# A planner of an attention block's engine order gets a new cost for changes of tiling, and its constants are refitted

## The chip, the cores and the metric

The kernel runs on one core of one Trainium2 chip. The metric is device time in microseconds (us); before the change it is 821.35, the median of three runs from 821.32 to 821.77. Profile times are those of one profiled execution, whose span is 820.3 us.

## The reference

One transformer block with adaptive layer norm. S = 2048 tokens, D = 640, 32 heads of 20 columns, an inner width F = 1536. The conditioning vector c gives six vectors of 640 (shift, scale and gate for each half of the block).

```python
mod = (silu(c) @ w_mod).reshape(1, 6, 1, -1)
sa, ca, ga, sb, cb, gb = (mod[:, i] for i in range(6))
h = layernorm(x) * (1 + ca) + sa
q, k, v = heads(h @ wqkv)                      # 32 heads of 20
p = softmax(einsum('bhqd,bhkd->bhqk', q, k) * 20 ** -0.5)
x = x + ga * (merge(p @ v) @ wo)
h = layernorm(x) * (1 + cb) + sb
x = x + gb * (((h @ w_gate) * (h @ w_up)) @ w_down)
```

The large part is the attention: 32 heads x 2048 x 2048 exponentials.

## The kernel before

**A planner in the kernel file.** Nothing of the order of instructions is written out by hand. `build_kernel` makes some thousands of `Task` objects (engine, assumed duration, dependencies, priority, gate, buffers to acquire), and `Sched.run` plays them forward in an assumed time: whenever an engine is free it takes the ready task of lowest priority number. `pick_pe` decides for TensorE (PE). The order that results is emitted as five fixed instruction streams with semaphore waits (`emit_program`). So a constant of the planner does no work on the chip; it moves instructions.

**Units of attention.** The queries are cut into `CHUNKS` of 512, 512, 512, 256 and 256; a chunk and a set of four heads are an item (8 items a chunk, 40 in all). A unit is one head, 128 keys and 512 queries (256 keys and 256 queries in the last two chunks). PE computes its scores into one PSUM bank (`unit_score_emits`, L1306): the head dimension lies on 32 rows of the array (row tile `32*s` for head s of the set), so units of different heads can share a pass and units of the same head can't. Then come the exponentials, in one of two ways:

- A units go to ScalarE (ACT), L1342: two units to an instruction, from group `HEADG` = 600 on alternately two and three. Two PSUM sets (banks 0 to 2, and 3 and 4) are used in turn, so the scores of a group wait until the exponential two groups back is done. The results go to the buffers PP, `NPS` = 4 of each of two kinds.
- D units go to VectorE (DVE) in quads of four: one L1366 each (scores to int16 in DB0), then three instructions for the quad (L1398, L1403, L1406) that make two terms in DSS, each of which goes through the PV product. `QUADS` says how many quads each item has. Their scores are attached to an A group (`d_attach`), up to `EAGER` units ahead of being due.

**PV products.** `pv_issue` (L1832) multiplies PP or DSS with the values, four heads side by side in column tiles, into one bank (`BPV`). An item's bank is read by DVE (the stream transpose L1486) before the next item may begin, and ends in the columns `OcT` and `Ocp` for the output projection.

**The rest of PE's work** is cut into rounds (`Round`): transposes of the normalised input (`hT_rounds`, L948), projections of K and Q (`kq_round`, L981, and `packed_round`, L1033), of V (`v_round`), and for each finished chunk the suffix: output projection (`op`), second layer norm on DVE and GpSimd, transposes (L1604), gate and up products (`g`, `u`), down projection (`dn`). Most of them record their matmuls in L827 (four column tiles) or L823 (the whole array, in the last chunk's suffix). They are slipped in between the scores by priority and gate (`need`, `K_LEAD`, `KD_LEAD`, `LATE_A`, `LATE_L`, `GATE_F`). Where the planner sees PE idle too long, it puts in a filler pass (L2101, L2103), an idle product[...].

**Changes of tiling.** Scores use row tiles (mode S), PV and most projections column tiles (mode P), transposes the whole array (mode X). `mode_start` adds the cost of a change of mode:

```python
def mode_start(mode, t):
    if sc.pe_mode is not None and sc.pe_mode != mode:
        return max(t, sc.pe_end + PE_SWITCH)
    return max(t, sc.pe_end)
```

**Stealing.** `Sched.steal` lets ScalarE take an evacuation from DVE's list when it sees no exponential due within `STEAL_GAP`, up to `STEAL_END`.

Of the kernel before, what the change touches and what calls it, by code (L numbers as in the profile page):

```python
# [14 lines left out]
PE_SWITCH = 100.0  # L15
# [10 lines left out]
STEAL_GAP = 188.158  # L26
# [402 lines left out]
QUADS = [(0, 4, 3, 3, 4, 3, 4, 3), (3, 4, 3, 4, 3, 4, 3, 4), (3, 4, 3, 4, 3, 4, 3, 4), (1, 2, 1, 2, 1, 2, 1, 2), 1]  # L429
# [3 lines left out]
EAGER = 4  # L433
# [5 lines left out]
PVTOL = 400  # L439
# [13 lines left out]
K_LEAD = 0.642  # L453
K_ALL = (0,)
KD_LEAD = 0.704
DMA_WINDOW = 900000
D_LATE = 12
D_RES = 84
# [4 lines left out]
TAILX = 1  # L463
PV0N = 1
# [13 lines left out]
HT_L = 0.046  # L478
V_L = 0.251
LATE_A = 1.114  # L480
LATE_L = 2.959
LATEQ = (3,)
LATEQ_A = 0
# [13 lines left out]
def build_kernel(nc, A_x, A_wqkv, A_wo, B_x, B_w_gate, B_w_up, B_w_down, c, w_mod, out):  # L497
# [265 lines left out]
    def load_rest():  # L763
        chain(load_w, d_wk, 0, 1, wk_sb, 0, "sp", 0.5)
        chained.append(d_wk[0])
        for q, f in enumerate((lambda: chain(load_x, 1, 0, "sp", 0.6), lambda: chain(load_w, d_wq, 0, 0, wq_sb, 0, "sp", 0.7),
                               lambda: chain(load_x, 1, 1, "sp", 0.8), lambda: chain(load_w, d_wv, 0, 2, wV, 0, "sp", 0.9),
                               lambda: chain(load_x, 2, 0, "sp", 4), lambda: chain(load_x, 2, 1, "sp", 4.1),
                               lambda: chain(load_x, 3, 0, "sp", 5), lambda: chain(load_x, 3, 1, "sp", 5.1),
                               lambda: chain(load_w, d_wk, 1, 1, wk_sb, 0, "sp", 8),  # L770
                               lambda: chain(load_w, d_wq, 1, 0, wq_sb, 0, "sp", 8.1),
                               lambda: chain(load_w, d_wv, 1, 2, wV, 0, "sp", 8.2))):
            n = len(sc.every)
            f()
            chained.append(sc.every[n])
# [17 lines left out]
    class Round:  # L793
        def __init__(self, mms, deps, after, prio, gate=0, name="", banks=None, pdeps={}):
# [11 lines left out]
            for i, (dur, f) in enumerate(mms):  # L806
                t = Task("pe", dur, wrap(f), deps if i == 0 else pdeps.get(i, ()), ctr="pex", prio=prio, gate=gate, name=name,
                         mode="P" if isinstance(f, list) else "X")
                if i > 0:
                    follower[id(self.tasks[-1])] = t  # L810
                self.tasks.append(t)
# [8 lines left out]
            self.evac[-1].on_start = lambda task: banks.done(b["b"], task)  # L820
# [120 lines left out]
    def hT_rounds(tc, prio):  # L941
        s2 = tc % 2
        t_hT[tc] = []
        tr_last[tc] = []
        for k in range(KD):
# [18 lines left out]
    kt_ready = {}  # L964
    qt_ready = {}
# [9 lines left out]

    def kq_round(kind, j, tc, prio, gate=0):
# [8 lines left out]
        pieces = [(ci, q0 % 512, n) for ci, (q0, n) in enumerate(CHUNKS) if q0 // 512 == tc]  # L985

        def after(r):
            if kind == "K":
                dps = [r_sb.last, r_cb.last] if j >= 4 else []
                f = lambda e: e.tensor_copy(KT[:, j, tc * 512:(tc + 1) * 512], bank(r.b["b"]))  # L990
                fa = lambda e: e.copy(KT[:, j, tc * 512:(tc + 1) * 512], bank(r.b["b"]))
                return [evac(512, ps_cost(512), f, fa, [r.last] + dps)]
            ts = []
            for ci, so, n in pieces:
                f = lambda e, ci=ci, so=so, n=n: e.tensor_scalar(QT[ci][:, j, :], ps[:, r.b["b"], so:so + n], qcol[:, 0:1],
                                                                 None, op0=ALU.mult)
                fa = lambda e, ci=ci, so=so, n=n: e.activation(QT[ci][:, j, :], ps[:, r.b["b"], so:so + n], AFT.Copy,
                                                               scale=qcol[:, 0:1])
                ts.append(evac(n, ps_cost(n), f, fa, [r.last] + d_q + (x0_done if ci > 0 else [])))
            return ts  # L1000
# [5 lines left out]
        r = Round(mms, list(t_hT[tc]) + w_deps(kind, j) + xd, after, prio, gate=gate, name=f"{kind}{j}.{tc}")  # L1006
        if kind == "K":
            kt_ready[(j, tc)] = [r.evac[0]]
        else:
            for (ci, so, n), t in zip(pieces, r.evac):  # L1010
                qt_ready[(j, ci)] = [t]
# [15 lines left out]
    def packed_round(kind, b, tc, prio, gate=0, late_q=False):  # L1027
# [24 lines left out]
        r = Round(mms, list(t_hT[tc]) + dw, after, prio, gate=gate, name=f"{kind}p{b}.{tc}")  # L1052
# [54 lines left out]
    def v_round(t, pt, prio, gate=0):  # L1107
# [14 lines left out]
        r = Round(mms, list(t_hT[t // 4]) + [d_wv[a // 4]], after, prio, gate=gate, name=f"V{t}.{pt}")  # L1122
# [174 lines left out]
    def unit_score_deps(u):  # L1297
        d = list(qt_ready[(u.j, u.ci)])
        for tc in sorted(set(kt // 4 for kt in u.kts)):
            d += kt_ready[(u.j, tc)]  # L1300
        return d
# [452 lines left out]
    def mode_start(mode, t):  # L1754
        if sc.pe_mode is not None and sc.pe_mode != mode:
            return max(t, sc.pe_end + PE_SWITCH)
# [82 lines left out]
    def pv_issue(cands, t):  # L1839
# [4 lines left out]
        w = 216.0 * clk()  # L1844
# [60 lines left out]
    def pick_x(t, warm=False):  # L1905
# [3 lines left out]
        if xcur[0] is not None:  # L1909
            cand = xcur[0]  # L1910
            if any(d.done is None or d.done + SEM > t for d in cand.deps):
                return False
# [12 lines left out]
        if cand is not None:  # L1925
# [8 lines left out]
            xcur[0] = follower.get(id(cand))  # L1934
            return True
# [46 lines left out]
    def pick_pe(t):  # L1982
# [67 lines left out]
        if cands:  # L2050
# [4 lines left out]
            if PVTOL and sr is not None and not force:  # L2055
                k = int((sr + PVTOL - mode_start("P", t)) // 216.0)
# [62 lines left out]
    def fill_ok(t, fdeps):  # L2119
        if any(d.done is None or d.done + SEM > t for d in fdeps):  # L2120
            return False
        if xcur[0] is not None:
            return False
# [3 lines left out]
    xcur = [None]  # L2127
    sc.pick_pe = pick_pe
# [47 lines left out]
```

## Time and profile before

| | before |
|---|---|
| time | 821.35 us (821.32 to 821.77) |
| span of the profiled run | 820.3 us, granted TensorE clock 1.00 |
| exponentials on ScalarE (L1342) | 779 instructions, the first at 15.9 us, the last ends at 785.5 us |
| scores (L1306) | 2560 matmuls |
| DVE's share of the exponentials | 400 units: 265.5 us in L1366, 121.9 in L1403, 69.7 in L1398, 68.0 in L1406 |
| filler passes in column tiles (L2103) | 244 matmuls, 21.6 us |

Busy times are of one execution. Matmuls overlap, so PE's busy time says that something was under way and not that the array was full; a matmul that is recorded with 0.39 us can follow the one before it by 0.22. An idle time in square brackets stands before the instruction and names who ended it. The exponentials of 1024 elements are recorded with 1124 ns on average, but overlap each other: their distance from start to start is what counts.

### The profile page before, as it was taken

The numbers are of one execution on the slowest core, as the hardware profiler recorded it, in microseconds if no ns is written. First come the engines' busy times: TensorE is split into PE (matmuls) and PEld (weight loads), VectorE is DVE, ScalarE is ACT, GpSimd is POOL, SyncE is SP. The second block draws the span as 40 slices with busy tenths as digits, with TensorE's granted clock in tenths as the row PEclk, the third lists the DMA queues.
The fourth block names the chain that finished last, engine by engine and source line by source line (L and its number), as shares of the span: only waits on it lengthen the run. The fifth ranks groups of instructions, "written<-read, shape, count | busy, mean of one in ns | idle before, by whom it ended". The sixth has DMA issues, their size and how long they took to land.

```text
span 820.3 us, 27666 instructions
## 1 busy us (share of the span) xinstructions
PE 796.5 (97%) x11894; PEld 297.1 (36%) x11894; DVE 727.9 (89%) x1276; ACT 775.6 (95%) x822; POOL 71.7 (9%) x104
## 2 busy tenths in 40 slices
PE   9999999999999999999999999999999999999998
PEld 4433233322232222223333222223344443454567
DVE  7889899999899999999999999999789898758663
ACT  6889999999999999999999999999999999999931
POOL 2300000000001000000002000000011000001000
PEclk9999999999999999999999999999999999999999
DMA  9452311124400125100310121100401226106420
GB/s 294 128 169 71 95 50 41 33 66 131 111 15 26 44 64 155 41 5 15 70 42 6 37 46 46 37 5 19 102 5 30 62 66 136 31 30 141 104 59 17
DMA packets 115895, 54.23 MB, mean 66 GB/s; under 512 B 83771, under 2 KB 115775, under 8 KB 115775
## 3 DMA queue, kind: packets, MB, share of 16 engines
q1 hardware_dynamic: 114847, 51.33, 24.4%
q8 instruction: 94, 1.54, 0.8%
q10 hardware_dynamic: 928, 1.15, 0.4%
q14 instruction: 26, 0.21, 0.1%
HBM read 41.75 MB, written 8.41 MB: 61 GB/s over the span
## 4 chain that ended last, share of the span: by engine, by line
PE 42%; ACT 35%; DVE 14%; issue 7%; DMA 1%; SPq 0%; POOL 0%; ACTq 0%; DVEq 0%; POOLq 0%
ACT PP L1342 35%; PE ps_all L1306 13%; PE ps_all L827 13%; PE ps_all L1832 9%; DVE DB L1366 5%; PE ps_all L823 3%; PE ps_all L1033 2%; DVE DSS L1403 1%; DVE DSS L1398 1%; DVE DSS L1406 1%; PE ps_all L2101 1%; DVE st L921 1%; PE ps_all L981 1%; DVE wd L1294 1%; DVE hprod L1690 0%
## 5 line engine op out<-in xcount | busy, mean ns | idle before, releaser
L1342 ACT ACTIVATE PP<-ps_all 128x1024 bf16<-128x1024 f32 (+1 forms) x779 | 756.5, 1166 | 7.8 <-PE ps_all L1306 4.9
L1306 PE MATMUL ps_all<-QT,KT 32*128 32x512 bf16 (+1 forms) x2560 | 320.6, 339 | 12.8 <-ACT PP L1342 7.9
L1366 DVE TENSOR_SCALAR DB<-ps_all 128x512 int16<-128x512 f32 x400 | 265.5, 684 | 32.1 <-PE ps_all L1306 30.3
L1306 PEld LDWEIGHTS ps_all<-QT,KT 32*128 32x128 bf16 x2560 | 85.3, 91 | 277.2 <-ACT PP L1342 239.3
L1832 PE MATMUL ps_all<-PP,Vf 128*32 128x512 bf16 (+2 forms) x2080 | 163.4, 343 | 0.1
L1403 DVE TENSOR_TENSOR DSS<-DB,DSS 128x2048 bf16<-128x2048 bf16 x100 | 121.9, 1219 | 0.0
L827 PE MATMUL ps_all<-h2T,stg 128*32 128x512 bf16 x1440 | 116.0, 382 | 1.1 <-DVE DB L1366 0.4
L1491 POOL TENSOR_TENSOR OTn<-OT,invT 128x512 bf16<-128x512 f32 (+1 forms) x39 | 39.7, 1017 | 617.6 <-DVE invT L1489 617.6
L1832 PE MATMUL ps_all<-DSS,Vf 128*32 128x512 bf16 (+1 forms) x960 | 78.7, 347 | 0.1
L1832 PEld LDWEIGHTS ps_all<-PP,Vf 128*32 128x32 bf16 (+1 forms) x2080 | 46.5, 94 | 87.2 <-issue 80.6
L1398 DVE TENSOR_SCALAR DSS<-DB 128x2048 int16<-128x2048 int16 x100 | 69.7, 697 | 0.7
L1406 DVE TENSOR_SCALAR DSS<-DB 128x2048 int16<-128x2048 int16 x100 | 68.0, 680 | 0.8 <-PE ps_all L1832 0.7
L827 PE MATMUL ps_all<-wd,hprod 128*32 128x320 bf16 x1152 | 58.4, 301 | 0.2 <-DVE DB L1366 0.2
L827 PEld LDWEIGHTS ps_all<-h2T,stg 128*32 128x32 bf16 x1440 | 31.1, 95 | 34.6 <-issue 23.2
L1679 DVE CAST gsb<-ps_all 128x512 bf16<-128x512 f32 (+1 forms) x48 | 29.7, 619 | 5.8 <-PE ps_all L827 5.4
L827 PEld LDWEIGHTS ps_all<-wd,hprod 128*32 128x32 bf16 x1152 | 27.2, 96 | 18.4 <-issue 8.8
L1832 PEld LDWEIGHTS ps_all<-DSS,Vf 128*32 128x32 bf16 x960 | 25.1, 95 | 20.6 <-issue 8.8
L827 PE MATMUL ps_all<-wV,hT 128*32 128x320 bf16 x640 | 31.4, 301 | 0.1
L1033 PE MATMUL ps_all<-hT,wq 128*32 128x512 bf16 x375 | 31.1, 382 | 0.0
L1486 DVE STREAM_TRANSPOSE OT<-ps_all 128x512 f32<-128x512 f32 (+1 forms) x40 | 24.3, 606 | 7.7 <-PE ps_all L1832 7.4
L827 PE MATMUL ps_all<-wo,Ocp 128*32 128x320 bf16 x560 | 30.6, 301 | 0.4 <-DVE DB L1366 0.4
L1498 DVE STREAM_TRANSPOSE OcT<-OTn 128x512 bf16<-128x512 bf16 (+1 forms) x40 | 23.8, 596 | 2.2 <-POOL OTn L1491 2.2
(123 smaller groups left out, 519.5 us busy)
## 6 DMA issues: line engine op xcount, KB each, us to landing
stg<-in_B_w_gate_dram SPq DMA_DIRECT2D x50, 160.0 KB, 2.8
stg<-in_B_w_up_dram SPq DMA_DIRECT2D x50, 160.0 KB, 3.0
QT<-q_rows SPq DMA_DIRECT2D x22, 128.0 KB, 2.9
KT<-k_rows SPq DMA_DIRECT2D x84, 32.0 KB, 1.7
wm<-in_w_mod_dram SPq DMA_DIRECT2D x3, 800.0 KB
x<-in_A_x_dram SPq DMA_DIRECT2D x7, 320.0 KB
xck<-in_A_x_dram SPq DMA_DIRECT2D x3, 640.0 KB
wd<-in_B_w_down_dram SPq DMA_DIRECT2D x1, 1920.0 KB
```

The source lines that it names most:

```text
L823: return lambda e, b: e.matmul(ps[:, b, c0:c0 + n], lhs(), rhs(), start=st, stop=sp)
L827: return lambda e, b: e.matmul(ps[32 * x:32 * x + 32, b, c0:c0 + n], lhs()[:, 32 * x:32 * x + 32], rhs(), tile_position=(0, 32 * x), start ...
L1033: f = [lambda e, b_, k=k, x=x: e.matmul(ps[x:x + min(32, w - x), b_, :], wx[:, k, r0 + x:r0 + min(x + 32, w)], hT[tc][:, k, :], tile_posit ...
L1306: ems.append(lambda e, i=i, kt=kt: e.matmul(dstf()[:, i * u.n:(i + 1) * u.n], KT[32 * u.s:32 * u.s + 32, u.j, kt * 128:(kt + 1) * 128], QT ...
L1342: return e.activation(PPs[g % 2][:, cellp["p"], 0:nu * 512], ps[:, b0:b0 + nu, :].rearrange("p b c -> p (b c)"), AFT.Exp, scale=ESCALE)
L1366: return e.tensor_scalar(DB0[:, st_["slot"], x * 512:(x + 1) * 512], bank(cell["b"]), EBIAS, 0.0, op0=ALU.add, op1=ALU.max)
L1398: return e.tensor_scalar(DSS[:, st_["ss"][0], :], DB0[:, st_["slot"], :], 0x7F, 0x3F00, op0=ALU.bitwise_and, op1=ALU.bitwise_or)
L1403: return e.tensor_tensor(d, DB0[:, st_["slot"], :].bitcast(BF16), d, ALU.mult)
L1406: return e.tensor_scalar(DSS[:, st_["ss"][1], :], DB0[:, st_["slot"], :], 0x7F80, 2, op0=ALU.bitwise_and, op1=ALU.bitwise_or)
L1491: f3 = lambda e: e.tensor_tensor(OTn[:, 0:n].rearrange("p (b c) -> p b c", c=32), OT[:, 0:n].rearrange("p (b c) -> p b c", c=32), invT[:, ...
L1679: f = lambda e: e.tensor_copy(gsb[:, gs, 0:n], ps[:, r.b["b"], 0:n])
L1832: ems.append(lambda e, i=i, kt=kt, stt=stt, stp=stp: e.matmul(ps[32 * s:32 * s + mc, BPV, 0:u.n], Vf[:, (kt * H + 4 * u.j + s) * VW:(kt * ...
```

## The change

The planner's cost of a change of tiling is split in two: leaving the scores' row tiles costs `PE_BACK` = 112 ns, any other change `PE_SWITCH` = 102 ns (both were 100). The duration of a pass of PV products becomes a constant (`PV_W`, still 216 ns), and an extra for the first pass of a round is prepared (`X_FIRST`, 0). Several new ways of ordering are built in and left off (`PASSDEP`, `WQ_FIRST`, `EV_SPLIT`, `HT0_SPLIT`, `PREEMPT`). One new path is live: when the next pass of a round that has begun is blocked, small `col` matmuls may go ahead of it. The other constants are fitted again to the planner so changed. Among them are two that change the work itself: the item pattern `QUADS` has two quads fewer in the fourth chunk (12 become 10), and in the second chunk the sixth item has one quad less and the seventh one more.

```diff
-PE_SWITCH = 100.0
+PE_SWITCH = 102.0
+PE_BACK = 112.0
+PV_W = 216.0
+X_FIRST = 0.0
...
-STEAL_GAP = 188.158
+STEAL_GAP = 138.041
...
-QUADS = [(0, 4, 3, 3, 4, 3, 4, 3), (3, 4, 3, 4, 3, 4, 3, 4), (3, 4, 3, 4, 3, 4, 3, 4), (1, 2, 1, 2, 1, 2, 1, 2), 1]
+QUADS = [(0, 4, 3, 3, 4, 3, 4, 3), (3, 4, 3, 4, 3, 3, 4, 4), (3, 4, 3, 4, 3, 4, 3, 4), (1, 2, 1, 2, 1, 1, 1, 1), 1]
...
-EAGER = 4
+EAGER = 7
...
-PVTOL = 400
+PVTOL = 300
...
-K_LEAD = 0.642
+K_LEAD = 0.686
 K_ALL = (0,)
-KD_LEAD = 0.704
+KD_LEAD = 0.64
 DMA_WINDOW = 900000
 D_LATE = 12
-D_RES = 84
+D_RES = 79
...
+PASSDEP = 0
+WQ_FIRST = 0
+EV_SPLIT = 0
+PASS_TC = (0, 1, 2, 3)
+HT0_SPLIT = 0
+PREEMPT = 0.0
+PRE_M = 0.3
...
-HT_L = 0.046
+HT_L = 0.11
 V_L = 0.251
-LATE_A = 1.114
-LATE_L = 2.959
+LATE_A = 2.37
+LATE_L = 2.957
 LATEQ = (3,)
-LATEQ_A = 0
+LATEQ_A = 4
...
-            return max(t, sc.pe_end + PE_SWITCH)
+            return max(t, sc.pe_end + (PE_BACK if sc.pe_mode == 'S' else PE_SWITCH))
...
-                k = int((sr + PVTOL - mode_start("P", t)) // 216.0)
+                k = int((sr + PVTOL - mode_start("P", t)) // PV_W)
```

## The prediction

> **What bounds the kernel now.** I read the page first, then the busy time of each engine by stretch, then the exponentials alone, then the waits and the timeline where the exponentials thin out. The page:
>
> ```profile
> PE 796.5 (97%) x11894; PEld 297.1 (36%) x11894; DVE 727.9 (89%) x1276; ACT 775.6 (95%) x822; POOL 71.7 (9%) x104
> ...
> PE 42%; ACT 35%; DVE 14%; issue 7%; DMA 1%; SPq 0%; POOL 0%; ACTq 0%; DVEq 0%; POOLq 0%
> ```
>
> PE looks like the bound, in busy time and in the chain that ended last. The waits say otherwise:
>
> ```profile
> PEld ps_all L1306 <- ACT PP L1342: 239.3, 639, 1.1
> ```
>
> 639 weight loads of score groups (0.37 us each on average) wait for ScalarE to let go of a PSUM pair. So over most of the span PE follows ScalarE. The exponentials by stretch (stretch, length, ACT busy, count):
>
> ```profile
> 16.00:72.00 56.00, 46.64 (x51) 1.00 0.49 143
> 72.00:119.00 47.00, 46.44 (x52) 1.00 0.31 79
> 119.00:166.00 47.00, 46.02 (x51) 1.00 0.14 40
> 166.00:560.00 394.00, 393.91 (x431) 1.00 0.19 50
> ...
> 680.00:780.00 100.00, 99.95 (x89) 1.00 0.41 90
> ```
>
> A stretch counts an exponential that straddles its edge, so I take one off. Undisturbed, one of two units starts every 0.904 us (the chain has six in 5.41 us at 220). From 16 to 72 some 50 start: 56 - 50 x 0.904 = 10.8 us lost. From 72 to 166 about 3 us are lost, from 166 to 560 394 - 430 x 0.904 = 5.3 us, or 1.4%. From 680 to 780, where groups of two and three units alternate, 88 start in 100 us, 0.45 us a unit. So ScalarE is the bound from about 70 to 785 us; before that it starves, and the timeline shows what it starves for, and one more hole later on:
>
> ```profile
> 37.17 7.44 ACT L1342 ACTIVATE PP<-ps_all 128x1024 bf16<-128x1024 f32 x8 [1.45 <-PE ps_all L1306]
> 45.47 3.77 ACT L1342 ACTIVATE PP<-ps_all 128x1024 bf16<-128x1024 f32 x4 [0.86 <-PE ps_all L1306]
> ...
> 621.30 79.82 ACT L1342 ACTIVATE PP<-ps_all 128x1024 bf16<-128x1024 f32 x70 [1.83 <-PE ps_all L1832]
> ```
>
> The first two are scores that PE brings late, behind projections. The third waits for PV products to free PP buffers, and PV waits for DVE to read the finished item out of its bank:
>
> ```profile
> 601.06 0.45 DVE L1486 STREAM_TRANSPOSE OT<-ps_all 128x256 f32<-128x256 f32 x1
> ...
> 620.34 0.45 DVE L1486 STREAM_TRANSPOSE OT<-ps_all 128x256 f32<-128x256 f32 x1
> ```
>
> Between these two item ends lie 19.3 us in which DVE hardly pauses. After the last exponential (785.5) PE works without a break to the end, but for one hole:
>
> ```profile
> 792.59 3.44 PE L827 MATMUL ps_all<-wd,hprodt 128*32 128x320 bf16 x96
> ...
> 795.96 0.73 PE L1604 MATMUL ps_all<-ident,xn2c 128*128 128x128 bf16 x10
> ```
>
> The gate product behind it waits 1.12 us for h2Tc and starts at 797.82.
>
> **What the Trainium skill says.** "ScalarE: Activation LUTs" (What ACT_TABLE_LOAD costs) gives 0.833 ns an element plus 186 ns, with 93 ns of overlap back to back: 946 ns for 1024 elements. The trace has 0.904 us, and I use the trace. "TensorE: Matmul & The Clock Gate" (The mechanism, in Part 3) lets matmuls at different row positions overlap in the array. The trace agrees: the scores of different row tiles cost one pass, while two units on one row tile cost a second one:
>
> ```profile
> 45.03 0.61 PE L1306 MATMUL ps_all<-QT,KT 32*128 32x512 bf16 x5
> 45.57 0.40 PE L1832 MATMUL ps_all<-PP,Vf 128*32 128x512 bf16 x4
> ...
> 46.77 0.39 PE L1306 MATMUL ps_all<-QT,KT 32*128 32x512 bf16 x3
> 47.09 0.73 PE L827 MATMUL ps_all<-wV,hT 128*32 128x320 bf16 x16
> ```
>
> From score start to next start: 0.54 us with five units, 0.32 with three, so 0.22 us a repeated pass. "TensorEngine Tiling (Array Packing)" (Key Properties) says that a change of tiling mode drains the array. 0.32 less a 0.216 us pass leaves about 0.1 us a change, as both planners assume.
>
> **The change part by part**, from the order of instructions in the two built programs and the durations above.
>
> *Constants of the switch, and switches left off.* The planner's costs set no instruction. The new paths (split evacuation, dependencies by pass, split transposes) are off, and changes of tiling number 1567 before and 1568 after. By themselves they cost 0: what counts is the order that comes out.
>
> *Two quads fewer in the fourth chunk.* Eight units move from DVE to ScalarE, 1648 + 400 becoming 1656 + 392: 691 exponentials of two units (689 before), 91 of three (90), one of one. 8 x 0.45 = **+3.6 us** on ScalarE, in a stretch in which it has no gap. DVE loses 2 x (4 x 0.684 + 1.219 + 0.697 + 0.680) = 10.7 us, off the path: ScalarE's exponentials hide it. PE loses two passes of PV, 0.4 us, hidden likewise.
>
> *Fewer repeated score passes.* 834 passes become 798: 36 x 0.216 = 7.8 us of PE. Most lie where ScalarE sets the pace (units 600 to 1400), and ten more filler passes there (71 against 61, 2.2 us) show that PE merely has more room. Groups with a repeated pass start their exponential only some 10 to 20 ns later than others do. Together with the quad moved from the sixth to the seventh item of the second chunk, where DVE is busy 39.89 of the 40 us from 320, I give the saturated stretch **-1.0 us** of its 5.3 (bounds 0 and 2.5).
>
> *Order of the head.* Up to the first PV the orders are the same. From there transposes, V and K projections are dealt differently. Adding pass times and 0.107 us a change of tiling ahead of each exponential, PE brings the 100th ScalarE unit 0.5 us earlier, the 160th to 270th 1.7 to 2.5 us, the 280th to 300th 1.0 to 1.3 us. PE sets the pace there, so ScalarE gains what PE does: **-2.0 us** (bounds 0.5 and 3).
>
> *The hole at 621.* Between the same two item ends DVE now has one DB evacuation less (0.68), one sum (0.48), one normalisation (0.44), one aggregation (0.2) and two h2T evacuations (1.0), which come after: 2.8 us less than 19.3. The PV products come that much earlier, and the hole of 1.83 closes: **-1.8 us** (bounds 0 and 1.8, as the same 28 PV products are still piled up behind it).
>
> *Tail.* 12 passes of down projection move from ahead of the output projection to between the transposes and the first gate product: 12 x 0.14 = 1.7 us that cover the 1.12 us hole and a little more. Queued behind them on PE are the gate products alone, which could not start anyway. From the last PV product to the first gate product there were 22 down passes (3.1), the output projection (3.4), 24 down passes (3.4), the transposes (0.6) and 1.2 of hole, 11.7 in all; now 2 up passes (0.2), 12 down, the output projection, 24 down, the transposes, 12 down, 11.0: **-0.7 us** (bounds -1.1 and 0).
>
> *Waits and releases.* ScalarE steals the same evacuations as before; two V evacuations now stand together (0.42 us each), while PE is the bound: 0.
>
> Sum: 3.6 - 1.0 - 2.0 - 1.8 - 0.7 = -1.9 us, so 821.35 - 1.9 = **819.4 us**.
>
> **The rivals.**
> (a) *Nearly no change*: the head gains only the 1.3 us of its latest late unit (280 to 300), the hole closes by half, the saturated stretch yields nothing: 3.6 - 1.3 - 0.9 - 0.7 = +0.7, 822.0. For it speaks that a wait which is removed early is paid again if a later unit is late.
> (b) *Slower*: exponentials are added for certain, and the stalls stay, since the same item end piles up the same 28 PV products and a second pile of 24 follows 26 units later where there was none: 3.6 - 0.7 - 0.5 = +2.4, 823.8. For it speaks that ScalarE is the bound by every stretch; against it, that DVE's work ahead of the pile is less.
> (c) *Larger gain*: PE is the bound after all, as the 97% suggest. Its counted work falls 7.8 + 0.4 - 2.2 = 6.0 us: 815.4. Against it speak the 639 waits for ScalarE.
>
> **How the numbers follow.** Forecast 0.40, (a) 0.23, (b) 0.24, (c) 0.13. Faster by over 0.2% (below 819.7) are the forecast and (c): 0.53. Slower (above 823.0) is (b): 0.24. The range runs from (c) to (b), 815.4 to 823.8; beyond it lie half of (c) on one side and less than half of (b) on the other. All single terms at their best or worst would give 816.5 and 824.5, and they will hardly all fall together.
>
> **What would show it.** Right: the last exponential ends about 784.3 (785.5 - 1.2), the count from 16 to 72 rises by one or two, no ScalarE gap over 1 us near 620, no PE hole ahead of the first gate product. Wrong: the same 10.8 us lost before 72, a gap near 620 as long as before or a new one some 12 us later, or exponentials in the saturated stretch further apart than 0.914 us, which would be ScalarE waiting on a PE that holds fewer, larger bundles.

## The result, and the profile after

The changed kernel takes **824.63 us** (median of six runs, 824.28 to 826.0) beside 821.66 (821.32 to 821.93) for the kernel before on the same chip: a ratio of 1.0038, 95% interval 1.0026 to 1.0051. It is slower by 0.26% to 0.51%, above the range of 815.4 to 823.8, where 819.4 had been forecast. The span of the profiled execution is 822.5 us, 2.2 more than before (the profiled execution of before was a run of 822.43 us, 0.8 above its median; that of after one of 824.28).

The page of the changed kernel, busy times and the chain that ended last:

```profile
PE 791.9 (96%) x11918; PEld 292.7 (36%) x11918; DVE 719.2 (87%) x1262; ACT 778.2 (95%) x826; POOL 77.7 (9%) x104
...
PE 41%; ACT 40%; DVE 11%; issue 7%; DMA 1%; ACTq 0%; DVEq 0%
```

and from its waits (us in total, times, longest) the largest of the score groups:

```profile
PEld ps_all L1373 <- ACT PP L1409: 259.4, 678, 0.9
```

PE is 4.6 us less busy, DVE 8.7 less, ACT 2.6 more, and 678 score loads instead of 639 wait for ScalarE. By these numbers PE has more room, and the kernel is slower. The exponentials by stretch (stretch, length, ACT busy, count):

```profile
16.00:72.00 56.00, 46.15 (x50) 1.00 0.49 144
72.00:119.00 47.00, 46.83 (x52) 1.00 0.28 74
119.00:166.00 47.00, 44.78 (x49) 1.00 0.15 43
...
560.00:621.00 61.00, 61.00 (x59) 1.00 0.15 37
621.00:680.00 59.00, 59.00 (x53) 1.00 0.25 56
```

Up to 166 us 151 exponentials against 154 before. Forecast was one or two more up to 72; there is one fewer. From 560 to 680 ScalarE is busy all 120 us: the hole is gone. ScalarE's timeline shows both, here the starved parts of the head and the last stretch:

```profile
58.12 1.94 ACT L1409 ACTIVATE PP<-ps_all 128x1024 bf16<-128x1024 f32 x2 [0.20 <-PE ps_all L1899]
60.55 1.94 ACT L1409 ACTIVATE PP<-ps_all 128x1024 bf16<-128x1024 f32 x2 [0.50 <-PE ps_all L1899]
...
151.32 1.94 ACT L1409 ACTIVATE PP<-ps_all 128x1024 bf16<-128x1024 f32 x2 [0.39 <-PE ps_all L1899]
154.28 1.02 ACT L1409 ACTIVATE PP<-ps_all 128x1024 bf16<-128x1024 f32 x1 [1.03 <-PE ps_all L1899]
...
482.58 305.16 ACT L1409 ACTIVATE PP<-ps_all 128x1024 bf16<-128x1024 f32 x290 [0.38 <-PE ps_all L1373]
```

In the last line 290 exponentials run on to 787.7 with no gap worth a line of its own. The waits of the head shown here have another releaser than the two shown of before: L1899 is the PV product, not the score product (L1373). ScalarE has its scores and waits for a PP buffer. Its waits over the first 166.5 us (us in total, times, longest), two lines of before and then two of after, say the same for the whole head:

```profile
ACT PP L1342 <- PE ps_all L1306: 4.9, 7, 1.4
ACT PP L1342 <- PE ps_all L1832: 0.5, 2, 0.3
...
ACT PP L1409 <- PE ps_all L1899: 4.1, 9, 1.0
ACT PP L1409 <- PE ps_all L1373: 3.2, 6, 1.4
```

The waits for scores fell by 1.7 us, about what was forecast for the head, and the waits for PV products rose by 3.6.

**The ledger.** I laid the start of every exponential of both traces side by side, by the ScalarE unit it begins with. The column "trace" is how much (after - before) grows over each part:

| part | forecast, us | trace, us |
|---|---|---|
| head, to unit 300 | -2.0 | +1.1 |
| units 300 to 1200, saturated | -1.0 | -0.1 |
| units 1200 to 1300, the hole | -1.8 | -1.9 |
| units 1300 to 1640 | 0 | -0.7 |
| from unit 1640 to the last exponential (785.5, now 787.7), with eight units more | +3.6 | +3.9 |
| tail, last exponential to the end (34.79, now 34.75) | -0.7 | 0.0 |
| sum | -1.9 | +2.2 |

Two terms failed, the head and the tail, and of a third, the saturated stretch, next to nothing is left. The experiments ask why.

### The profile page after: what moved, and what is told of

Its sections match the earlier page's. It is cut to its first block, busy times and chain, and to the rows that moved or that the text cites. A ratio compares the mean times of both kernels' runs of the same rounds, so it can differ in the third digit from the quotient of the medians.

```text
span 822.5 us, 27752 instructions
## 1 busy us (share of the span) xinstructions
PE 791.9 (96%) x11918; PEld 292.7 (36%) x11918; DVE 719.2 (87%) x1262; ACT 778.2 (95%) x826; POOL 77.7 (9%) x104
## 4 chain that ended last, share of the span: by engine, by line
PE 41%; ACT 40%; DVE 11%; issue 7%; DMA 1%; ACTq 0%; DVEq 0%
ACT PP L1409 40%; PE ps_all L1373 13%; PE ps_all L845 12%; PE ps_all L1899 9%; DVE DB L1433 4%; PE ps_all L841 3%; PE ps_all L1096 2%; DVE DSS L1470 1%; DVE DSS L1465 1%; PE ps_all L1034 1%; DMA wm<-in_w_mod_dram 1%; DVE DSS L1473 1%; DVE OT L1553 0%; DVE Vf L1183 0%; PE ps_all L1671 0%
## 5 line engine op out<-in xcount | busy, mean ns | idle before, releaser
L1373 PE MATMUL ps_all<-QT,KT 32*128 32x512 bf16 (+1 forms) x2560 | 311.7, 340 | 17.8 <-ACT PP L1409 14.5
L1433 DVE TENSOR_SCALAR DB<-ps_all 128x512 int16<-128x512 f32 x392 | 260.0, 681 | 35.7 <-PE ps_all L1373 34.0
L1373 PEld LDWEIGHTS ps_all<-QT,KT 32*128 32x128 bf16 x2560 | 82.1, 91 | 285.5 <-ACT PP L1409 259.4
L1899 PE MATMUL ps_all<-PP,Vf 128*32 128x512 bf16 (+2 forms) x2096 | 164.9, 342 | 0.0
L845 PE MATMUL ps_all<-h2T,stg 128*32 128x512 bf16 x1440 | 113.7, 382 | 1.9 <-DVE gsb L1746 1.1
L1558 POOL TENSOR_TENSOR OTn<-OT,invT 128x512 bf16<-128x512 f32 (+1 forms) x39 | 44.5, 1140 | 600.8 <-DVE invT L1556 596.3
L1899 PEld LDWEIGHTS ps_all<-PP,Vf 128*32 128x32 bf16 (+1 forms) x2096 | 47.3, 94 | 87.0 <-issue 81.1
L1899 PE MATMUL ps_all<-DSS,Vf 128*32 128x512 bf16 (+3 forms) x928 | 77.4, 350 | 0.4 <-DVE DSS L1473 0.2
L845 PE MATMUL ps_all<-wd,hprod 128*32 128x320 bf16 x1152 | 59.3, 301 | 1.8 <-DVE DB L1433 1.5
L845 PEld LDWEIGHTS ps_all<-h2T,stg 128*32 128x32 bf16 x1440 | 31.2, 95 | 31.4 <-issue 16.7
L845 PEld LDWEIGHTS ps_all<-wd,hprod 128*32 128x32 bf16 x1152 | 27.2, 96 | 19.1 <-issue 8.9
L845 PE MATMUL ps_all<-wV,hT 128*32 128x320 bf16 x640 | 31.8, 301 | 0.1
L1899 PEld LDWEIGHTS ps_all<-DSS,Vf 128*32 128x32 bf16 (+1 forms) x928 | 23.8, 95 | 22.0 <-issue 11.2
L1096 PE MATMUL ps_all<-hT,wq 128*32 128x512 bf16 x375 | 30.8, 382 | 0.2 <-DVE DB L1433 0.2
L845 PE MATMUL ps_all<-wo,Ocp 128*32 128x320 bf16 x560 | 30.6, 301 | 0.3
L1553 DVE STREAM_TRANSPOSE OT<-ps_all 128x512 f32<-128x512 f32 (+1 forms) x40 | 24.1, 603 | 6.7 <-PE ps_all L1899 6.4
L1757 DVE TENSOR_TENSOR hprod<-ps_all,gsb 128x512 bf16<-128x512 f32 x36 | 24.6, 683 | 5.7 <-PE ps_all L845 5.6
```

What stands on the lines that cost most here:

```text
L845: return lambda e, b: e.matmul(ps[32 * x:32 * x + 32, b, c0:c0 + n], lhs()[:, 32 * x:32 * x + 32], rhs(), tile_position=(0, 32 * x), start ...
L1096: f = [lambda e, b_, k=k, x=x: e.matmul(ps[x:x + min(32, w - x), b_, :], wx[:, k, r0 + x:r0 + min(x + 32, w)], hT[tc][:, k, :], tile_posit ...
L1373: ems.append(lambda e, i=i, kt=kt: e.matmul(dstf()[:, i * u.n:(i + 1) * u.n], KT[32 * u.s:32 * u.s + 32, u.j, kt * 128:(kt + 1) * 128], QT ...
L1433: return e.tensor_scalar(DB0[:, st_["slot"], x * 512:(x + 1) * 512], bank(cell["b"]), EBIAS, 0.0, op0=ALU.add, op1=ALU.max)
L1558: f3 = lambda e: e.tensor_tensor(OTn[:, 0:n].rearrange("p (b c) -> p b c", c=32), OT[:, 0:n].rearrange("p (b c) -> p b c", c=32), invT[:, ...
L1899: ems.append(lambda e, i=i, kt=kt, stt=stt, stp=stp: e.matmul(ps[32 * s:32 * s + mc, BPV, 0:u.n], Vf[:, (kt * H + 4 * u.j + s) * VW:(kt * ...
```

## The experiments

All medians stand beside runs of the kernel before on the same chip (821.9; for the last four kernels 822.2). Two cautions for every profile below. Executions of one order differ by about 1 us already at the 10th unit, depending on when the first loads land. At unit 10 the profiled execution of *old_head* is +1.0 against before (its VectorE waits 0.96 us for x), of *before_new_quads* +0.9 and of *before_to_400* +0.5 (w_mod lands at 8.5 us instead of 7.9), of *after_values_early* +0.6. I compare steps behind that point.

And in five of the fourteen profiled executions the granted TensorE clock is at half for one stretch of 3.41 us, as here in *before_to_400* (stretch, length, PE busy, granted clock, DMA share, GB/s):

```profile
655.98:659.39 3.41, 2.69 (x50) 1.00 0.49 107
659.39:662.81 3.42, 3.42 (x40) 0.50 0.32 94
```

The other four: *after_q4_old* from 71.07, *before_switch_costs* from 100.18, *after_old_quads* from 627.42, *before_new_quads* from 801.59. Before and after show none. One such stretch is a mean clock of 0.998, and three of the 27 runs of before beside *after_q4_old* have that: they took 823.96 to 824.17 us, where the median is 821.94. In four of the five PE was busy for only 0.6 to 2.7 of the 3.41 us ahead of the stretch, in *after_q4_old* for 3.3; what brings it on was not tested.

### Which part of the order costs: the head exchanged

In the next two kernels the planner reads one set of constants up to score group 150 (unit 300) and the other from there; the new path for blocked rounds is on only where it reads those of after.

```diff
+HYB = 150
+HEAD_C = {'PE_SWITCH': 100.0, 'PE_BACK': 100.0, 'EAGER': 4, 'PVTOL': 400, 'D_RES': 84, 'STEAL_GAP': 188.158}
+REST_C = {'PE_SWITCH': 102.0, 'PE_BACK': 112.0, 'EAGER': 7, 'PVTOL': 300, 'D_RES': 79, 'STEAL_GAP': 138.041}
...
+        globals().update(HEAD_C if g < HYB else REST_C)
```

*old_head* is after with the head of before (K_LEAD, KD_LEAD, HT_L, LATE_A and LATE_L are those of before too); the diff shows it:

> The kernel after, planned up to group 150 (ScalarE unit 300) with the constants of the kernel before, so that all engines have the order of before up to there; from there on its own constants and its own quads. Theory of the ledger (ScalarE sets the pace; the head of the change lost 1.1 us by unit 300, because the last value projections come later and the item that needs them ends later): unit 300 starts at about 166.1 us as before, not at 167.2, and the time is 824.6 - 1.1 = 823.5 us. Rival (the time depends on the accident of the whole order; no part has a price of its own): unit 300 at 166.1 too, but the rest falls out anew, anywhere from 820 to 827 us.

Measured 823.76 us, ratio 1.0021 (1.0014 to 1.0028), as forecast: 0.9 less than after, or 1.1 when each is taken against before on its own chip (+1.9 and +3.0). From unit 10 to unit 300 it takes 144.57 us; before takes 144.61, after 146.0. *new_head* is before with the head of after, with the two sets exchanged (and K_LEAD, KD_LEAD, HT_L, LATE_A and LATE_L of after):

> The reverse: the kernel before, planned up to group 150 with the constants of the kernel after (order of after up to unit 300), then with its own constants and its own quads. Ledger: unit 300 at 167.2 us, time 821.7 + 1.1 = 822.8 us, the hole near 620 us as in before. Rival: unit 300 at 167.2, the rest anew, 819 to 826 us.

Measured 824.84, ratio 1.0033 (1.002 to 1.0046), a miss: more than forecast. Unit 300 starts at 167.91, 1.8 later than in before. But the rest didn't stay as it was: its hole closes only half, and its tail is 35.85 us instead of 34.79. From unit 10 its head takes 2.2 us more than that of before (146.76 us). The other kernels that have one of these two orders up to unit 300, instruction by instruction, agree: from unit 10 to unit 300 the six with the order of before take 144.6 to 145.0 us; of the five with that of after, four take 146.0 to 146.8, and *after_q4_old*, with its half clock from 71.07, takes 147.8. So the head of after costs 1.0 to 2.2 us at full clock, in either company; and the exchange of one part deals later parts again.

### The head: what the value projection holds up

An item's PV products need all V tiles of its half (`v_round`). If the last V tile comes late, PV products pile up, PP stays full, and ScalarE waits (L1899 above). VectorE's and PE's timeline of after around 154 us:

```profile
154.44 0.49 DVE L1183 CAST Vf<-ps_all 128x320 bf16<-128x320 f32 x1 [1.09 <-PE ps_all L845]
154.99 0.39 PE L1899 MATMUL ps_all<-PP,Vf 128*32 128x512 bf16 x1
156.34 0.71 DVE L1553 STREAM_TRANSPOSE OT<-ps_all 128x512 f32<-128x512 f32 x1
```

and the same two VectorE instructions of before:

```profile
153.09 0.49 DVE L1119 CAST Vf<-ps_all 128x320 bf16<-128x320 f32 x1
...
155.23 0.71 DVE L1486 STREAM_TRANSPOSE OT<-ps_all 128x512 f32<-128x512 f32 x1
```

VectorE waits 1.09 us for PE's V products (L845) before the last tile. That tile of the second half is 1.35 us later than in before, the end of the fifth item 1.1 us. In the first half it is 60.0 us instead of 58.2. The exponentials follow both: counted from unit 10, after is 0.9 us behind before at unit 60, level with it at unit 160, and 1.4 behind at unit 280. The time from the end of that last tile to the start of unit 300 hardly changes over seven kernels whose tile ends between 153.5 and 159.3 us:

| kernel | last V tile ends, us | unit 300 starts, us | between |
|---|---|---|---|
| before_q4_new | 153.53 | 166.06 | 12.5 |
| before | 153.58 | 166.11 | 12.5 |
| old_head | 154.54 | 167.09 | 12.6 |
| after | 154.93 | 167.22 | 12.3 |
| new_head | 155.35 | 167.91 | 12.6 |
| after_values_early | 155.89 | 169.21 | 13.3 |
| before_switch_costs | 159.30 | 172.04 | 12.7 |

In the other seven kernels it is 12.3 to 12.9 us. To test the mechanism, the V projections of after are given an earlier due time:

```diff
-V_L = 0.251
+V_L = 0.05
```

> The kernel after with V_L 0.05 instead of 0.251: the rounds of the value projection come forward. By pass times the last V tile of the first half comes 3.4 us earlier on PE (48.8 instead of 52.2 in the count), that of the second half 0.4 us earlier. Theory (in the head ScalarE waits for PP buffers, these for PV, and PV for the last V tile): the first item ends at about 58 us instead of 61.0, the four waits for PV between 56 and 65 us shrink from 2.0 us to under 1, ScalarE unit 100 starts about 1 us earlier than the 72.5 of after, unit 280 about as late as there; time 823.6 us or, if the rest falls out otherwise, 822 to 826. Rival (ScalarE waits in the head for scores, so for projections of K and Q): those come later now, and unit 100 starts at 72.5 us or later.

Measured 826.83, ratio 1.006 (1.0045 to 1.0075): slower, not faster. (The profiled execution, 825.65, is the fastest of four and the only one with a full clock.) Unit 100 starts at 72.89 us, later than in after, as the rival said; counted from unit 10 it is 0.5 us earlier, where 1 had been forecast. But the wait that it was to remove is removed. ScalarE's timeline of it, at both places:

```profile
38.33 7.44 ACT L1409 ACTIVATE PP<-ps_all 128x1024 bf16<-128x1024 f32 x8 [1.67 <-PE ps_all L1373]
...
49.13 41.42 ACT L1409 ACTIVATE PP<-ps_all 128x1024 bf16<-128x1024 f32 x45 [2.71 <-PE ps_all L1373]
...
154.46 4.93 ACT L1409 ACTIVATE PP<-ps_all 128x1024 bf16<-128x1024 f32 x5 [2.85 <-PE ps_all L1899]
```

From 49.13 on 45 exponentials run on without a wait for PV (after has four such waits in that time). The price stands ahead of them, 2.71 us of waiting for scores, and behind: the second half's last V tile comes no earlier (133.8 us after unit 10, in after 133.7), ScalarE is there 0.7 us sooner, and waits 2.85 us for PV. Up to 166.5 us its waits for scores are 6.4 us (in after 3.2), those for PV 3.3 (4.1). So the mechanism holds, and the constant is a trade: V products that come earlier on a full PE go with scores that come later.

### The two quads, alone and with their order

*after_old_quads* is after with all of before's pattern:

```diff
-QUADS = [(0, 4, 3, 3, 4, 3, 4, 3), (3, 4, 3, 4, 3, 3, 4, 4), (3, 4, 3, 4, 3, 4, 3, 4), (1, 2, 1, 2, 1, 1, 1, 1), 1]
+QUADS = [(0, 4, 3, 3, 4, 3, 4, 3), (3, 4, 3, 4, 3, 4, 3, 4), (3, 4, 3, 4, 3, 4, 3, 4), (1, 2, 1, 2, 1, 2, 1, 2), 1]
```

> The kernel after with the quads of the kernel before (12 in the fourth chunk, old pattern in the second): eight units go back from ScalarE to DVE. Ledger: 8 x 0.45 = 3.6 us less, 821.0 us; the ScalarE units before the fourth chunk start at the times of after within 0.5 us. Rival (DVE's relief is what closed the hole near 620 us, so the quads pay for themselves): the hole comes back and the time is 823 to 825 us.

Measured 827.61, ratio 1.0062 (1.0047 to 1.0077): both expectations missed, and the hole near 620 stays closed. Eight exponential units fewer, and 3 us more. Its ScalarE waits 1.02 us for PV at 366 and 0.87 for scores at 630, the second in its half-clock stretch, and its tail is 38.66 us. PE's timeline of its end shows what is in the tail (behind the last score group at 785.12):

```profile
788.07 2.23 PE L845 MATMUL ps_all<-h2Tt,stg 128*32 128x256 bf16 x68
...
793.72 1.82 PE L845 MATMUL ps_all<-h2Tt,stg 128*32 128x256 bf16 x60
...
798.49 5.07 PE L845 MATMUL ps_all<-wd,hprodt 128*32 128x320 bf16 x144
```

These are up and down products of the fourth chunk that no exponential covers any more: 180 matmuls of gate and up products (45 passes of four) where after has 40 (10 passes). *before_new_quads* is the reverse, before with all of after's pattern:

> The kernel before with the quads of the kernel after: eight units go from DVE to ScalarE and nothing else. Ledger: 821.7 + 3.6 = 825.3 us, hole near 620 us unchanged, as the two quads lie behind it. Rival (DVE's relief pays): the hole closes and the time is 823.5 us or less.

Measured 826.42, ratio 1.0048 (1.0031 to 1.0065), 1.1 more than forecast, and not by its ledger. The last exponential ends at 789.80 (+4.3, of which 0.9 is the start-up), but the hole that was to stay is closed (-2.0 from unit 1200 to 1300), units 300 to 1200 take 1.4 more, and the tail is 1.2 longer, with a half-clock stretch in it. Its one run with a full clock took 824.74. Two more kernels take the fourth chunk's pattern alone. *after_q4_old* gives after the old fourth tuple, *before_q4_new* gives before the new one:

> The kernel after with the old pattern in the fourth chunk alone (12 quads; the second chunk keeps its new pattern), so that the order up to the fourth chunk stays that of after. Refined ledger (the time is the end of the last exponential plus a tail; the tail is 34.8 us while the passes of the fourth chunk's suffix that are left after the last score group are no more than the 7.8 us that the last chunk's own chain can hide, and grows by what is more): last exponential 3.6 us earlier, about 784.2, but 29 up passes and 48 down passes left, 3.2 + 6.7 = 9.9 us, so a tail of 36.9 and 824.6 - 3.6 + 2.1 = 823.1 us. Rival (a unit costs ScalarE 0.45 us and that is all): 821.0 us with a tail of 34.8.

> The kernel before with the new pattern in the fourth chunk alone (10 quads), order up to the fourth chunk as before. Refined ledger: last exponential 3.6 us later, about 789.1; 35 down passes left (4.9 us), less than the chain hides, so the tail stays at 34.8 and the time is 821.7 + 3.6 = 825.3 us. Rival (less work left after the last exponential shortens the tail by 2.9 us): 822.4 us.

*after_q4_old* measured 823.23, ratio 1.0017 (1.0008 to 1.0026), as forecast: its exponentials end 1.9 us earlier than those of after, although its profiled execution was 1.7 us behind at unit 300 after its half-clock stretch, and 1.8 us come back in the tail (36.57). *before_q4_new* measured 823.10, ratio 1.0012 (1.0005 to 1.002): less than forecast and more than its rival. Its order (up to 653 us) and its times (up to unit 1400) are those of before. Then the last exponential is 2.85 us later and the tail 1.46 shorter (33.33). So the price of the eight units is real, +3.7 us from unit 1640 to the last exponential, but more than half of it comes back: 0.8 between units 1400 and 1640, and 1.5 in the tail, for which fewer down passes are left.

### What is left over for the end

This suggests a count: behind the last score group, how many up passes (gate and up products, 0.11 us each) and down passes (0.14) are still to come in the program, in kernels that have the same fixed rest (output projection, second norm, last chunk's products)?

| kernel | up + down passes left | us | 34.8 + (us - 7.8) | tail measured |
|---|---|---|---|---|
| before | 10 + 48 | 7.8 | 34.8 | 34.79 |
| after | 10 + 48 | 7.8 | 34.8 | 34.75 |
| old_head | 10 + 48 | 7.8 | 34.8 | 34.73 |
| after_values_early | 10 + 48 | 7.8 | 34.8 | 34.73 |
| before_to_620 | 19 + 48 | 8.8 | 35.8 | 35.36 |
| new_head | 25 + 48 | 9.5 | 36.4 | 35.85 |
| after_q4_old | 29 + 48 | 9.9 | 36.9 | 36.57 |
| before_to_400 | 29 + 48 | 9.9 | 36.9 | 36.84 |
| before_switch_costs | 30 + 48 | 10.0 | 37.0 | 36.61 |
| after_repeats | 35 + 48 | 10.6 | 37.5 | 37.53 |
| after_old_quads | 45 + 48 | 11.7 | 38.6 | 38.66 |
| before_nudged | 50 + 48 | 12.2 | 39.2 | 39.54 |
| before_q4_new | 0 + 35 | 4.9 | 31.9 | 33.33 |
| before_new_quads | 0 + 27 | 3.8 | 30.8 | 35.95 |

From 7.8 us up the count gives the tail within 0.6 us, whichever change brought it there. Below, it fails: PE runs out of left-over work and waits for the second norm. (In *before_new_quads* the half clock adds to this: from the first gate product to the end it takes 24.1 us, before 22.5.) In *before_q4_new*, with a filler pass ahead (L2103):

```profile
796.16 0.39 PE L2103 MATMUL ps_all<-ident 128*32 128x512 bf16 x4
797.69 0.73 PE L1604 MATMUL ps_all<-ident,xn2c 128*128 128x128 bf16 x10 [1.14 <-DVE xn2c L1593]
```

After has the same left-over as before, and the same tail. The first two lines are PE's timeline of before (its last PV product and the start of the output projection), the others that of after from its last PV product on:

```profile
785.91 0.39 PE L1832 MATMUL ps_all<-PP,Vf 128*32 128x256 bf16 x8
...
789.23 0.85 PE L823 MATMUL ps_all<-wo,Ocp 128*128 128x320 bf16 x5
...
787.81 0.40 PE L1899 MATMUL ps_all<-PP,Vf 128*32 128x256 bf16 x8
788.03 0.40 PE L845 MATMUL ps_all<-h2Tt,stg 128*32 128x256 bf16 x8
789.10 1.81 PE L845 MATMUL ps_all<-wd,hprodt 128*32 128x320 bf16 x48 [0.67 <-DVE hprodt L1757]
790.84 0.85 PE L841 MATMUL ps_all<-wo,Ocp 128*128 128x320 bf16 x5
...
794.21 3.44 PE L845 MATMUL ps_all<-wd,hprodt 128*32 128x320 bf16 x96
797.58 0.73 PE L1671 MATMUL ps_all<-ident,xn2c 128*128 128x128 bf16 x10
798.25 1.81 PE L845 MATMUL ps_all<-wd,hprodt 128*32 128x320 bf16 x48
800.00 11.09 PE L841 MATMUL ps_all<-h2Tc,stx 128*128 128x256 bf16 x100
```

The 12 down passes at 798.25 do fill the hole ahead of the gate products. They take more than it had: from the start of the transposes to the first gate product 2.42 us, where before has 1.86. That was to be more than made up ahead of the output projection, where 10 down passes fewer stand. But there a new hole of 0.67 us stands at 788.4, since the down products now wait for DVE to finish the last hprodt, and from the last PV product to the output projection it is 3.03 us instead of 3.32, where 1.2 less had been forecast.

### Does TensorE's room turn into time? Repeated score passes

In *after_repeats* the D units of groups 160 to 519 are attached, where possible, to a group that already uses their row tile: 165 repeated passes in the program instead of 32.

```diff
-            for u in dst["left"]:
-                if (u.s not in rows or relax) and all(d.done is not None and d.done + SEM <= t for d in unit_score_deps(u)):
+            for u in sorted(dst["left"], key=lambda x: 160 <= pvstate["sidx"] < 520 and x.s not in rows):
+                if (u.s not in rows or relax or 160 <= pvstate["sidx"] < 520) and all(d.done is not None and d.done + SEM <= t for d in unit_score_deps(u)):
```

> The kernel after, in which groups 160 to 519 take a D unit on a row tile that is already in use where there is one: 165 repeated score passes in the whole program instead of 32, 133 x 0.216 = 28.7 us more work on PE, 19 filler passes fewer. ScalarE sets the pace: the exponentials of those groups start 10 to 15 ns later, 1.3 to 2 us in all, and as 35 up passes (3.9 us) and the 48 down passes are left at the end, 2.8 us more of tail: about 829 us. Rival (PE is the bound, as its 96% say): 24.6 us more, about 849 us.

Measured 836.75, ratio 1.0181 (1.0164 to 1.0198), nearer to the first theory than to the one of a bound PE, and 7.8 above it. 133 passes more are 28.7 us of PE at 0.216. Between units 300 and 1200 ScalarE lost 15.5 us against its floor of 0.904 a group where after loses 6.5: 9.0 us, 68 ns a pass. The tail takes 2.8 (35 up passes left). Taken one by one, the 146 groups with a repeated pass in that stretch start their exponential 70 ns late on average, the 304 others 15. So ScalarE sets the pace there, as forecast, but a repeated pass isn't free: about a third of it reaches the exponentials.

### A nudge of the planner, and the new costs alone

*before_switch_costs* is the title's change by itself, in the kernel before:

```diff
-PE_SWITCH = 100.0
+PE_SWITCH = 102.0
+PE_BACK = 112.0
...
-            return max(t, sc.pe_end + PE_SWITCH)
+            return max(t, sc.pe_end + (PE_BACK if sc.pe_mode == 'S' else PE_SWITCH))
```

> The kernel before with the title's two switch costs alone, 102 ns into scores and 112 out of them, where it had 100 for both; quads and all other constants as before. Theory 'left-over work and the V tiles': left over after the last score group 30 up and 48 down passes, 10.0 us against 7.8, so tail 37.0 (+2.2); last V tile of the second half behind unit 278 by the program (before 274, after 278), so unit 300 at about 167.2 (+1.1) as in after. Sum 821.9 + 2.2 + 1.1 = 825.2 with the hole at 621 open, 823.4 with it closed. Rival 'the better costs are worth something by themselves': below 821.

*before_nudged* is, for comparison, before with a nudge of half a nanosecond:

```diff
-PE_SWITCH = 100.0
+PE_SWITCH = 100.5
```

> The kernel before with one planner cost nudged, 100.0 to 100.5 ns for a change of tiling; same quads, nothing else. The nudge means nothing for the chip, but the order is dealt again from the 12th score product on. Left over on TensorE after the last score group: 50 up and 48 down passes (12.2 us) where before has 10 and 48 (7.8). Theory 'what counts is where the deal leaves the projections, and what it leaves for the end': no exponential more, head within 0.5 us, tail 34.8 + 4.4 = 39.2, so 821.9 + 4.4 = 826.3, give or take 1.5 for the holes. Rival 'an order with the same quads and the same kind of plan costs the same': 821.9, give or take 0.8.

The costs alone: 829.9 us, ratio 1.0095 (1.0076 to 1.0114), more than forecast. The tail was right (36.61, forecast 37.0), the head far too good: unit 300 comes 5.9 us late. PE's timeline and ScalarE's show two waits:

```profile
100.06 0.54 PE L1308 MATMUL ps_all<-QT,KT 32*128 32x512 bf16 x3 [2.85 <-DMA QT<-q_rows]
...
100.64 1.02 ACT L1344 ACTIVATE PP<-ps_all 128x1024 bf16<-128x1024 f32 x1 [2.66 <-PE ps_all L1308]
...
159.43 2.86 ACT L1344 ACTIVATE PP<-ps_all 128x1024 bf16<-128x1024 f32 x3 [1.92 <-PE ps_all L1834]
```

The first is one I hadn't thought of: the queries of an item come through a DMA that was issued at 96.87 us (in before at 94.24), so late that PE stood idle for it. Behind it lies the half-clock stretch, and in it two more waits for scores, 0.50 and 0.75 us. The second is the V tile again. All four runs of this kernel have a mean clock of 0.996 to 0.998.

The nudge: 829.44 us, ratio 1.0082 (1.0058 to 1.0107), more than forecast. Its profiled execution has a span of 825.0, at the lower end of its runs. Its last exponential ends at 785.49, as in before to 0.02 us, and all that its trace lost is in the tail: 39.54 where 39.2 was forecast. On the way there the hole at 621 closed and a new one opened, by the same mechanism. VectorE, PE and ScalarE:

```profile
364.10 0.71 DVE L1487 STREAM_TRANSPOSE OT<-ps_all 128x512 f32<-128x512 f32 x1
...
364.86 0.83 PE L1833 MATMUL ps_all<-PP,Vf 128*32 128x512 bf16 x12 [0.24 <-DVE OT L1487]
365.31 1.02 ACT L1343 ACTIVATE PP<-ps_all 128x1024 bf16<-128x1024 f32 x1 [1.54 <-PE ps_all L1833]
```

Its runs lie 826.9 to 831.0, wider than those of the other kernels. Their granted clocks say why, in the main: it is 1.000 in the runs of 826.86 and 828.4 us and 0.994 in those of 830.48 and 831.03. At full clock, then, it is 0.6 and 2.1 us above the 826.3 that was forecast, give or take 1.5. Half a nanosecond costs as much as the two new costs do. So the new costs are not shown to be worse, or better: both deals give up what the constants of before had found, and the whole change, refit and quads together, gets back more than half of the loss (from 1.0095 to 1.0038).

### Before's order first, after's constants late

If head and left-over are what cost, before's quads and order with after's constants from the middle on should keep the head and close the hole. The switch as above (its six constants and the new path; K_LEAD to LATEQ_A stay those of before), at group 400 or 620, with before's QUADS:

> The kernel before, with its quads; from score group 400 (ScalarE unit 800) on the planner uses after's constants. Head is that of before. Left over after the last score group: 29 up and 48 down passes, 9.9 us: tail 36.9 (+2.1). Theory (ledger): with the hole closed 821.9 - 1.8 + 2.1 = 822.2, with it open 824.0. If both this and the version that changes at group 620 come out below 821.5, after's constants are better from the middle on and only its head and its eight more units cost.

> The kernel before, with its quads; from score group 620 (ScalarE unit 1280, some 20 units ahead of the hole) on the planner uses after's constants. Head and middle are those of before. Left over after the last score group: 19 up and 48 down passes, 8.8 us against 7.8: tail 35.8. Theory (ledger): with the hole closed 821.9 - 1.8 + 1.0 = 821.1, with it open 822.9. Rival 'a hole that closes is paid for elsewhere before the end': 822.9 with the hole closed.

*before_to_400* measured 822.14, ratio 0.9996 (0.9988 to 1.0005), as forecast. The hole at 621 is closed, and the tail is 36.84 (forecast 36.9). ScalarE's timeline:

```profile
588.80 72.82 ACT L1414 ACTIVATE PP<-ps_all 128x1536 bf16<-128x1536 f32 x64
662.46 29.06 ACT L1414 ACTIVATE PP<-ps_all 128x1536 bf16<-128x1536 f32 x25 [0.84 <-PE ps_all L1378]
```

It gains 1.9 us from unit 1200 to 1300 and gives 1.3 back by unit 1400, with the wait for scores at 662. That wait lies in the half-clock stretch shown above, so it is more likely this execution's than the order's: 11 of the 12 runs have a full clock, and the profiled one, 823.32, is the slowest. *before_to_620* measured 822.71, ratio 1.0005 (0.9997 to 1.0014), with the hole open as in before, so as forecast for that case:

```profile
621.64 19.12 ACT L1414 ACTIVATE PP<-ps_all 128x1024 bf16<-128x1024 f32 x17 [1.87 <-PE ps_all L1904]
```

What closes the hole is thus dealt before group 620, in DVE's list ahead of the item's end: between the two item ends DVE is busy 15.7 us in *before_to_400*, as in after, and 18.6 in *before_to_620*, as in before. Neither kernel is measurably faster than before, and no version that I ran beats it.

## Why the prediction was wrong

Of the 5.2 us between forecast and result 0.3 is the start (821.35 was the median of three runs of before, 821.66 that of six). The rest lies in the terms.

**Units, +3.6: right.** Eight more units took 3.9 us from unit 1640 to the last exponential. *before_q4_new*, with the order of before up to unit 1400, has 2.85 by its last exponential.

**The hole at 621, -1.8: right.** -1.9, by the step named. The two item ends in after:

```profile
602.49 0.44 DVE L1553 STREAM_TRANSPOSE OT<-ps_all 128x256 f32<-128x256 f32 x1
...
619.29 0.45 DVE L1553 STREAM_TRANSPOSE OT<-ps_all 128x256 f32<-128x256 f32 x1
```

Between them lie 16.8 us instead of 19.3, with 15.7 us of DVE work instead of 18.6 (2.8 less had been forecast). *before_to_400* and *before_to_620* differ in this list and in the hole in the same way. That a closed hole stays closed wasn't so certain: *before_nudged* closes this one and opens another at 365.

**Order of the head, -2.0: the step that failed.** "PE sets the pace there, so ScalarE gains what PE does" adds pass times ahead of each exponential's scores. It follows one of two chains. The other goes from the last V tile through the PV products to the PP buffers; there the same PE passes, in an order that serves the scores sooner, serve V later. PE's tally brought units 160 to 270 earlier by 1.7 to 2.5 us. Counted from unit 10, the trace has units 160 to 250 at most 0.2 us earlier, and unit 280 1.4 us later: ScalarE waits 1.7 us less for scores and 3.6 more for PV products. Rival (a) named the kind of event, "a wait which is removed early is paid again if a later unit is late", but still kept 1.3 us of gain.

**The saturated stretch, -1.0: the gain came and was lost again.** -0.1. By the two programs 38 groups of this stretch have a repeated pass in before and 11 in after. Laid beside the traces, these groups start their exponentials late by 1.0 us in all in before and by 0.05 in after, so a gain of 0.9 us is there, about what was forecast. But the other groups lose 6.5 us where before has 5.7. The term put that at nothing, and each deal has stalls of its own (the one at 365 appears in two kernels and in neither before nor after). (The 5.3 of 394 us that the prediction gives as lost there are 1.3%, not 1.4.)

**The tail, -0.7: the step that failed.** The 12 down passes do cover the hole of 1.12 us. But the sum of 11.7 against 11.0 added PE's own queue and took it to run without another wait; it measures 11.9 against 12.2. It lacked DVE's hprodt, which now opens a hole of 0.67 us ahead of the output projection. The count of left-over passes is the same in both kernels, and so is the tail; the passes were only moved within it.

**The rivals.** (b), 823.8, was nearest: exponentials added for certain, stalls not gained back. Its reason was another: the stall at 621 was to stay and a second pile of PV products to follow it, and neither is in the trace. (c) is refuted by *after_repeats*: on a bound PE the 133 repeated passes would have cost 24.6 us (28.7, less 19 filler passes), and 9.0 are seen between units 300 and 1200. The range failed at its upper end because it let no term turn its sign: a head bounded at -0.5 to -3 was the best case of a chain, and its worst, a later V tile, wasn't asked for.

What stays open: which step of the new order makes the small stalls of the saturated stretch; and what brings on the stretches at half clock. The 0.8 us between the difference of medians (3.0) and of the two profiled spans (2.2) is the choice of executions: that of before took 822.43, 0.8 above its median.

## What to carry to other kernels

A change of a planner's constants is a change of order, and its price is not in the constants: follow in the two programs each chain that can hold the bound engine (scores, values and the buffers that wait for them, loads), and take the latest, not the one that moved. Count what the order leaves behind the last instruction of the bound engine; here that count gave the tail within 0.6 us in the twelve of fourteen kernels that left at least as much as before (eight of them more), and it can be had without a run. Before you credit a refit, nudge a constant by next to nothing: here half a nanosecond moved the time by 0.8% (0.6 to 0.8% in its two runs at full clock), more than the whole change. And look at the granted clock of the execution that you profile before you read a stall as the order's.

## What the runs showed that I had not expected

- Work taken off ScalarE can lengthen the kernel: *after_old_quads* has 3.6 us of exponentials less than after and takes 3.0 us more.
- A repeated score pass costs the pace 68 ns of its 216 where many were added; in before a group that has one is 26 ns late on average. "TensorE: Matmul & The Clock Gate" (The mechanism, in Part 3) explains why scores on different row positions share a pass; what a pass more costs a kernel that another engine paces, only the run tells.
- One fixed order of instructions starts up to 1 us earlier or later in different executions, by the landing of its first loads, and keeps that shift long: *before_new_quads* is 0.9 us behind before at unit 10 and 1.1 at unit 600.
- A wait inside a stretch of 3.41 us at half clock looks like one of the order: 0.84 us in *before_to_400*, 0.87 in *after_old_quads*. Only the granted clock beside it tells.
